# Attention kernel: causal zeros in two parts on GpSimd, and a background rate that depends on what runs

## The chip, the core and the metric

The kernel runs on one core of a Trainium2 chip. A core has five engines with queues of their own: TensorE (PE; its weight loads are shown as PEld), VectorE (DVE), ScalarE (ACT), GpSimd (POOL) and SyncE (SP, which only issues transfers here). Each works through its queue in order and waits on semaphores for the others. The metric is the device time of one execution in microseconds (us); lower is better.

## The reference, cut to what matters

Two results stand side by side in the output. The right half is a spectral filter (a 2-D real FFT of a 2048 x 576 input, a product with complex weights, the inverse FFT). The left half is an attention with a memory over four segments of 512 rows, 32 heads of 18:

```python
for s in range(N):                      # N = 4 segments of L = 512 rows
    qs, ks, vs = q[:, :, s], k[:, :, s], v[:, :, s]
    logits = jnp.einsum("bhqd,bhkd->bhqk", qs, ks) * scale + mask   # causal
    p = _softmax(logits, axis=-1)
    a_dot = jnp.einsum("bhqk,bhkd->bhqd", p, vs)
    pq = phi(qs)
    num = jnp.einsum("bhld,bhde->bhle", pq, M)                      # memory terms
    den = jnp.einsum("bhld,bhd->bhl", pq, z)[..., None] + 1e-6
    o = g * (num / den) + (1.0 - g) * a_dot
    ...
    M = M + jnp.einsum("bhld,bhle->bhde", phi(ks), vs)
    z = z + jnp.einsum("bhld->bhd", phi(ks))
return o @ wo
```

## The kernel before, in words

The first 350 us or so hold the forward FFT, the projections to q, k and v, and the inverse FFT. The change touches only the last stage, `attention`.

`attention` runs 133 steps; step t handles one head of one segment. Four heads make a quad (k = t // 4, place hh = t % 4), two quads a head group (n = k // 2), eight groups of steps, 32 in all, a segment. In a step the program writes, in this order and in alternation:

- `s1(t+11)`: the logits of the head 11 steps ahead, in three PSUM tiles, only for the row maxima (VectorE: `mg`, `mx`);
- `s2(t)`: the logits of head t, transposed, with the maxima subtracted through two added rows of the query stack; ScalarE's exponentials (L728, L733, L737) write P[0], P[1], P[2];
- `pv`: the products of the quad before with v, half of them at hh = 1 (P[0] and the last 128 columns of P[1]), half at hh = 3 (the rest of P[1], and P[2]);
- background pieces by `run_bg`, from a list of generators.

When a quad's last exponentials are issued (hh = 3), GpSimd sets the part above the diagonal to zero in four blocks (`sel`, L741). At the next step (hh = 0) `mpath` prepares the maxima of the quad two ahead: VectorE and ScalarE put them into `mg`, GpSimd splits them into two bf16 parts `mh` (L707, L708), TensorE transposes those one step later (`mt`, L711), ScalarE copies them and issues the transfer that writes them into the query stack (L717). Query stacks (Qs) stand in three buffers, key stacks in four; their transfers go out on SyncE's queue, one or two a step.

The background consists of `late_setup` (the output weight wo: SyncE loads a block into `ob`, ScalarE copies it into `woh`, GpSimd writes the rest `wol`, L650), the denominators `den` (pd, L807 and L810), `mixed` (for each of five tiles a combining piece of the segment before, L878 with VectorE's product and, from the second segment on, GpSimd's add L884; a memory piece `pn` L831; a piece `pb` L837) and `oproj` (the output projection `po`, L901, in 16 half units). All of these take their PSUM tile from one bank (`post`). `run_bg(rate)` adds the rate to an account and runs one piece when the account has reached 1; it is called twice a step, with 0 and with 1.2, so that every fifth step has two pieces. `later(k, f)` puts f at the end of the step k - 1 after the present one, seen from within a step.

The order in which instructions are written is the order of each engine's queue: nothing reorders them. The tile framework adds the semaphore waits. Transfers issued by SyncE and ScalarE use eight semaphores in turn, and each waits for the one that had its semaphore before.

Of the kernel before, what the change touches and what calls it, by code (L numbers as in the profile page):

```python
# [5 lines left out]
F32=mybir.dt.float32; F32R=mybir.dt.float32r  # L6
# [402 lines left out]
class ATT:  # L409
# [223 lines left out]
    def late_setup(s,cp):  # L633

        nc,io=s.nc,s.io; q=[]
        s.sel=cp.tile([96,5,126],BF,name="sel",bufs=1); nc.gpsimd.dma_start(s.sel,io["sel"].rearrange("p (t m) -> p t m",t=5))
        s.woh=cp.tile([128,5,576],F32R,name="woh",bufs=1); s.wol=cp.tile([128,5,576],F32R,name="wol",bufs=1)
        for t in (0,1,2,3,5,4,6):
            if t: yield
            if t<6:  # L640
                x=cp.tile([128,576],F32,name="ob"); q.append((t,x))
                nc.sync.dma_start(x,io["wo"][:,576*t:576*t+576])
            yield
            if t!=5: yield
            if len(q)>(t<6):
                u,x=q.pop(0)
                if u==5: nc.scalar.copy(s.wol[64:96,4],x[64:96]); continue
                r=128 if u<4 else 72
                nc.scalar.copy(s.woh[:,u],x)
                nc.gpsimd.tensor_tensor(s.wol[:r,u],x[:r],s.woh[:r,u].bitcast(F32),op=OP.subtract)  # L650
        yield
        yield from s.gates()
    def stack_dmas(s,n,qk):
# [65 lines left out]
    def s2(s,t):  # L719
        nc=s.nc; k,hh=divmod(t,4); n,qd=divmod(k,2); h=4*qd+hh  # L720
        Q,K=s.Qs[n%3],s.Ks[n%4]; tp=s.tp
        if hh==0: s.P[k]=[tp.tile([128,4,w],F32,name=f"P{i}") for i,w in enumerate((512,512,256))]
        P=s.P[k]
        q=lambda o: Q[:110,h,o:]
        kk=lambda j: K[:110,h,128*j:128*j+128]
        p0=s.ps.tile([128,512],F32,name="s2",tag="s2")
        nc.tensor.matmul(p0,kk(0),q(0),start=True,stop=True)  # L727
        nc.scalar.activation(P[0][:,hh],p0,AF.Exp,scale=SC)  # L728
        yield
        p1=s.ps.tile([128,512],F32,name="s2",tag="s2")  # L730
        nc.tensor.matmul(p1[:,:384],kk(1),q(128),start=True,stop=True)  # L731
        nc.tensor.matmul(p1[:,384:],kk(3),q(384),start=True,stop=True)  # L732
        nc.scalar.activation(P[1][:,hh],p1,AF.Exp,scale=SC)  # L733
        yield
        p2=s.ps.tile([128,256],F32,name="s2",tag="s2")
        nc.tensor.matmul(p2,kk(2),q(256),start=True,stop=True)  # L736
        nc.scalar.activation(P[2][:,hh],p2,AF.Exp,scale=SC)  # L737
        r=slice(0,4) if k<31 else (slice(0,3) if hh==2 else slice(3,4))
        if hh==3 or k==31 and hh==2:
            def sel(x):  # L740
                nc.gpsimd.affine_select(out=x[:,r],in_=x[:,r],pattern=[[0,r.stop-r.start],[1,128]],compare_op=OP.is_ge,fill=0.0,base=0,channel_multiplier=-1)  # L741
            sel(P[0][:,:,:128])
            sel(P[1][:,:,:128])
            sel(P[1][:,:,384:])
            sel(P[2][:,:,:128])
        yield
    def pv(s,k,jj):

# [91 lines left out]
        yield  # L840
    def mixed(s,g):

        c=s.combine(g-1)
        d=5 if g==3 else 4
        for i in range(5+d):
            next(c,None); yield
            if i>=d:
                for _ in s.mem1(g,ORD[i-d]): yield
    def ux_load(s,g,t):
        r=126 if t<4 else 72  # L850
        s.ux[t]=s.tp.tile([128,512],F32,name="ux",tag="ux",bufs=3)
        s.nc.sync.dma_start(s.ux[t][:r],s.uD[g][126*t:126*t+r])
    def combine(s,g):

        nc=s.nc; tp=s.tp; xs=s.ux
        s.oh=[None]*5; s.ol=[None]*5
        eng=lambda: nc.vector if s.now>=117 else nc.gpsimd
        yield
        yield
        def high(u):  # L860
            r=126 if u<4 else 72
            s.oh[u]=tp.tile([128,512],F32R,name="oh",bufs=5); s.ol[u]=tp.tile([128,512],F32R,name="ol",bufs=5)
            (nc.vector.tensor_copy if s.now>=119 else nc.scalar.copy)(s.oh[u][:r],s.am[u][:r])
        def low(u):
            r=126 if u<4 else 72
            A,B=s.oh[u],s.ol[u]
            l=B if u<4 else tp.tile([128,512],F32R,name="ol4",bufs=1)
            eng().tensor_tensor(l[:r],s.am[u][:r],A[:r].bitcast(F32),op=OP.subtract)
            if u==4:
                s.later(1,lambda: nc.sync.dma_start(B[:72].bitcast(F32),A[:72].bitcast(F32)))  # L870
                s.later(2,lambda: (nc.sync.dma_start(A[72:128].bitcast(F32),l[:56].bitcast(F32)),nc.sync.dma_start(B[72:88].bitcast(F32),l[56:72].bitcast(F32))))
        late=g==2
        for t in range(7+late):
            if t>1 and not late: high(ORD[t-2]); low(ORD[t-2])
            if t<5:
                i=t; t=ORD[t]; r=126 if t<4 else 72; x=xs[t]
                pb=s.post("pb")
                nc.tensor.matmul(pb[:r],s.sel[:,t,:r],s.rc["rr"],start=True,stop=True)  # L878
                if g==0:
                    s.am[t]=tp.tile([126,512],F32,name="am",bufs=5)  # L880
                    nc.vector.tensor_tensor(s.am[t][:r],x[:r],pb[:r],op=OP.mult)
                else:
                    nc.vector.tensor_tensor(x[:r],x[:r],pb[:r],op=OP.mult)
                    eng().tensor_tensor(s.am[t][:r],x[:r],s.am[t][:r],op=OP.add)  # L884
                t=i
                if t<2: s.later(1,lambda t=t: s.ux_load(g,ORD[t+3]))
            if late and 1<t<7: high(ORD[t-2])
            if late and t>2: low(ORD[t-3])
            yield
# [49 lines left out]
    def begin(s,sm,sp,ps1):  # L939
        s.late=[]; s.now=-1  # L940
        s.sm,s.sp,s.ps1=sm,sp,ps1
        s.mh=sm.tile([128,8,16],BF,name="mh",bufs=1); s.nc.gpsimd.memset(s.mh,0.0)
        s.mg={};s.mx={};s.m2={};s.P={};s.vs={};s.rc={};s.am={};s.pq={};s.ux={};s.potag=None
    def prologue(s):

        nc,io=s.nc,s.io
# [18 lines left out]
    def attention(s,tp,ps):  # L965
        nc=s.nc; s.tp,s.ps,s.psm,s.mtag=tp,ps,s.ps1,"s1"
# [18 lines left out]
        for t in range(133):  # L985
            k,hh=divmod(t,4); n,qd=divmod(k,2); g=k//8
            if hh==0 and qd==0:
                if 0<n<14: q+=s.stack_dmas(n+2,0)
                if 0<n<13: q+=s.stack_dmas(n+3,1)
                if n+2<16: q.append(lambda n=n: s.load_v(n+2))  # L990
            st=t%32
            if 16<=t<21: s.pq_load(1,ORD[t-16])
            if t==34: bg.append(s.den(1,lane))
            if st==8 and g>0:
                def ln(g=g):
                    r=s.recip(s.rD[g-1],s.rrD[g-1],s.g1,False,"rr",2)
                    for i in range(8):
                        if 2<i<6: s.ux_load(g-1,ORD[i-3])
                        next(r); yield
                    yield from r  # L1000
                    bg.append(s.mixed(g))
                    o=s.oproj(g-1)
                    if g<3: bg.append(itertools.islice(o,4)); bg.append(s.den(g+1,lane))
                    bg.append(o)
                lane.append(ln())
            if t==125: lane.append(s.recip(s.rD[3],s.rrD[3],s.g1,False,"rr"))
            a=s.s1(t+11) if t+11<128 else iter(())
            b=s.s2(t) if t<128 else iter(())
            if q: q.pop(0)()
            if qu: qu.pop(0)()  # L1010
            steps(a,1)
            steps(b,1)
            run_bg(0)
            steps(a,1)
            steps(b,1)
            if 4<=t-1<132: s.pv((t-5)//4,(t-5)%4)
            run_bg(1.2)
            steps(a,1)
            if hh==1 and m is not None: steps(m,1)
            steps(b,1)  # L1020
            if hh==1 and m is not None: steps(m,1)
            if hh==0 and k+2<32: m=s.mpath(k+2); next(m)
            if t>=7 and t%4==3:
                s.pv_out((t-7)//4)
                if t%8==3:
                    u=s.u_dmas((t-11)//8)
                    if t<124: s.later(1,lambda u=u: qu.extend(u))
                    else: qu+=u
            for l in list(lane):
                try: next(l)  # L1030
                except StopIteration: lane.remove(l)
            if q and t%8==0: q.pop(0)()
            if qu: qu.pop(0)()
            s.due(t)
# [32 lines left out]
        nc=s.nc  # L1067
# [113 lines left out]
```

## Time and profile before

| | |
|---|---|
| median of 3 runs | 703.1 us (702.56 to 704.32) |
| profiled execution | 701.82 us, span 700.1 us |
| clock granted to TensorE | 1.00 |
| attention steps | from about 352 us to the end |
| busy, share of the span | PE 97%, PEld 72%, DVE 77%, ACT 63%, POOL 28% |
| DMA | 123.81 MB, mean 177 GB/s |

The span is the time from the program's first to its last instruction; the execution's own time holds 1.7 us more. In the rows, "out<-in" are the program's tile names, the numbers in front are start and length in us (timeline) or a total, a count and the longest (waits), and what stands in brackets is the idle time before an instruction and what ended it. Idle time of an engine that nobody waits for costs nothing.

### The profile page before, as it was taken

What the parts mean: (1) busy time and instruction counts of PE and PEld (TensorE: products, weight loads), DVE (VectorE), ACT (ScalarE), POOL (GpSimd) and SP (SyncE); (2) the same over time, 40 slices, a digit from 0 to 9 for tenths busy, and PEclk for the clock granted to TensorE, in tenths of its full rate; (3) what the DMA queues carried; (4) which work ended last, traced back from release to release, by engine and by line L of the source; (5) the groups of instructions that cost most, each with busy time, mean ns of one, the idle gap of its engine ahead of it and who ended that gap; (6) DMA issues with size and microseconds to landing.
All of it is one profiled execution on the core that took longest, in us unless ns stands there. A gap on an engine that the chain in (4) does not pass through costs nothing.

```text
span 700.1 us, 14377 instructions
## 1 busy us (share of the span) xinstructions
PE 682.6 (97%) x5040; PEld 502.6 (72%) x5040; DVE 537.1 (77%) x1149; ACT 444.5 (63%) x997; POOL 192.7 (28%) x389
## 2 busy tenths in 40 slices
PE   9999999999999999999999999999999999998998
PEld 6899779879879879999954445445666445664497
DVE  5799979779689679788688888888657876567633
ACT  4677795585685483554378787777666776567531
POOL 2111000100100102655225343443323652235310
PEclk9999999999999999999999999999999999999999
DMA  9896455585466678899338976976666766442152
GB/s 342 273 287 184 134 162 188 166 240 172 122 183 206 163 199 296 196 241 265 126 113 198 200 169 148 202 199 158 151 134 170 196 166 153 101 132 68 28 153 90
DMA packets 71362, 123.81 MB, mean 177 GB/s; under 512 B 12236, under 2 KB 39530, under 8 KB 67698
## 3 DMA queue, kind: packets, MB, share of 16 engines
q1 hardware_dynamic: 64638, 106.89, 57.7%
q0 software_dynamic: 5632, 15.76, 8.1%
q8 instruction: 40, 0.66, 0.4%
q10 hardware_dynamic: 1020, 0.25, 0.2%
q14 instruction: 32, 0.26, 0.1%
HBM read 82.10 MB, written 39.81 MB: 174 GB/s over the span
## 4 chain that ended last, share of the span: by engine, by line
PE 76%; DVE 7%; DMA 6%; ACT 5%; issue 2%; POOL 2%; SPq 1%; ACTq 0%; DVEq 0%; POOLq 0%
PE s L678 10%; PE pj L485 10%; PE pv L756 10%; PE pjv L485 7%; PE po L901 6%; PE i L330 4%; PE i L319 4%; PE f L145 4%; PE s L727 3%; PE c L166 3%; PE s L731 3%; PE po L930 2%; PE pn L831 2%; PE s L691 2%; PE s L736 2%
## 5 line engine op out<-in xcount | busy, mean ns | idle before, releaser
L686 DVE CUSTOM_DVE_ANT_0 junk<-s,x 128x512 bf16<-128x512 f32 x248 | 136.8, 551 | 55.8 <-PE s L678 50.7
L741 POOL TENSOR_SCALAR_AFFINE_SELECT P<-P 128x512 f32<-128x512 f32 (+2 forms) x132 | 78.3, 625 | 110.1 <-ACT P L728 102.2
L692 DVE TENSOR_REDUCE mx<-s 128x4 f32<-128x512 f32 x128 | 87.6, 684 | 5.2 <-PE s L691 3.3
L728 ACT ACTIVATE P<-s 128x512 f32<-128x512 f32 x128 | 77.9, 608 | 10.3 <-PE s L727 3.1
L756 PE MATMUL pv<-P,vs 128*32 128x512 f32 (+3 forms) x1024 | 82.5, 439 | 0.1
L737 ACT ACTIVATE P<-s 128x256 f32<-128x256 f32 x128 | 50.0, 390 | 46.9 <-PE s L736 46.5
L733 ACT ACTIVATE P<-s 128x512 f32<-128x512 f32 x128 | 77.7, 607 | 2.4 <-PE s L732 2.2
L678 PE MATMUL s<-Ks,Qs 108*128 108x384 bf16 (+3 forms) x256 | 69.2, 301 | 1.6 <-DVE mx L692 1.2
L756 PEld LDWEIGHTS pv<-P,vs 128*32 128x32 f32 x1024 | 26.9, 109 | 45.3 <-issue 34.8
L485 PE MATMUL pj<-x,wqkh 128*128 128x512 f32 x162 | 56.3, 408 | 0.0
L231 DVE TENSOR_TENSOR Z<-Z 128x580 f32<-128x580 f32 (+2 forms) x51 | 45.9, 911 | 0.5
L678 PEld LDWEIGHTS <-Qs 108*128 108x128 bf16 x320 | 31.5, 98 | 19.1 <-issue 8.7
L691 PE MATMUL s<-tri,idb 128*128 128x128 bf16 x256 | 43.0, 219 | 0.0
L543 POOL MEMSET vt<- 128x32 f32 x16 | 2.4, 162 | 140.7 <-PE pm L553 122.8
L319 PE MATMUL i<-civ,Y 128*128 128x256 f32 (+1 forms) x288 | 39.4, 289 | 0.6 <-POOL Y L304 0.6
L504 DVE SCALAR_TENSOR_TENSOR ex<-pj,ex 128x512 f32<-128x512 f32 (+1 forms) x28 | 19.3, 688 | 24.7 <-ACT ex L502 24.7
L319 PEld LDWEIGHTS i<-civ,Y 128*128 128x128 f32 (+1 forms) x288 | 36.6, 181 | 1.6 <-POOL Y L304 1.0
L330 PE MATMUL i<-itab,T 128*128 128x290 f32 (+1 forms) x224 | 36.7, 307 | 0.1
L485 PE MATMUL pj<-xh,wqkl 128*128 128x512 f32 x90 | 35.6, 395 | 0.0
L485 PE MATMUL pj<-x,wqkl 128*128 128x512 f32 x90 | 35.6, 395 | 0.0
L485 PE MATMUL pj<-xh,wqkh 128*128 128x512 f32 x90 | 35.6, 395 | 0.0
L485 PEld LDWEIGHTS pj<-x,wqkh 128*128 128x128 f32 x162 | 30.5, 189 | 6.5
(216 smaller groups left out, 1808.1 us busy)
## 6 DMA issues: line engine op xcount, KB each, us to landing
qkD<-sp SPq DMA_DIRECT2D x32, 384.0 KB
xin<-xb SPq DMA_DIRECT2D x16, 384.0 KB
cfw<-cfw POOLq DMA_DIRECT2D x16, 384.0 KB, 4.2
civ<-civ POOLq DMA_DIRECT2D x16, 384.0 KB, 9.1
vs<-vD SPq DMA_DIRECT2D x16, 330.0 KB
vD<-vt SPq DMA_DIRECT2D x16, 311.0 KB
W<-w SPq DMA_DIRECT2D x16, 290.0 KB
yb<-yout SPq DMA_DIRECT2D x16, 290.0 KB
```

The costliest lines, as they stand in the source:

```text
L319: nc.tensor.matmul(p[:m,k],Y[i][:,q,c*128:c*128+m],cc[:,hl,o:o+256],start=n==0,stop=n==5)
L330: nc.tensor.matmul(p,x,t,start=n==0,stop=n==6)
L485: s.nc.tensor.matmul(out,a,b,start=i==0,stop=i==len(L)-1)
L678: nc.tensor.matmul(out,Q[:108,h,128*i:128*i+128],K[:108,h,:128*(i+1)],start=True,stop=True)
L686: nc.vector.tensor_tensor_reduce(out=junk[:,:w],in0=src,in1=s.mask[:,512-w:],scale=1.0,scalar=-3.0e38, op0=OP.add,op1=OP.max,accum_out=s.m ...
L691: nc.tensor.matmul(pa[:,o+w-128:o+w],s.idb,s.tri,start=False,stop=True,skip_group_check=True)
L692: nc.vector.tensor_reduce(out=s.mx[k][:,hh],in_=pa.rearrange("p (b c) -> p b c",c=128),axis=mybir.AxisListType.X,op=OP.max)
L728: nc.scalar.activation(P[0][:,hh],p0,AF.Exp,scale=SC)
L733: nc.scalar.activation(P[1][:,hh],p1,AF.Exp,scale=SC)
L737: nc.scalar.activation(P[2][:,hh],p2,AF.Exp,scale=SC)
L741: nc.gpsimd.affine_select(out=x[:,r],in_=x[:,r],pattern=[[0,r.stop-r.start],[1,128]],compare_op=OP.is_ge,fill=0.0,base=0,channel_multiplie ...
L756: nc.tensor.matmul(s.pvt[32*hh:32*hh+32,128*j:],vt[:,j,19*h:19*h+32],mv[0][:,hh,mv[1]],start=j==0,stop=j>1,skip_group_check=True)
```

## The change

Four edits. Two of a quad's four zeros (the first 128 columns of P[1], and P[2]) are written at the end of the next step, behind the two parts of the maxima; the last quad keeps all four together. The subtraction for `wol` goes to the end of its step, and `late_setup` has one piece more for each of five blocks. The add on GpSimd in the combining piece goes to the end of the step where that step is the first of a quad, for the second segment only. The background's rate is 1.0 while `mixed` runs for segments 1 and 2, 1.35 after that, and 1.2 before the first and from the last one on.

```diff
                 nc.scalar.copy(s.woh[:,u],x)
-                nc.gpsimd.tensor_tensor(s.wol[:r,u],x[:r],s.woh[:r,u].bitcast(F32),op=OP.subtract)
+                s.later(1,lambda u=u,x=x,r=r: nc.gpsimd.tensor_tensor(s.wol[:r,u],x[:r],s.woh[:r,u].bitcast(F32),op=OP.subtract))
+                yield
...
             sel(P[0][:,:,:128])
-            sel(P[1][:,:,:128])
             sel(P[1][:,:,384:])
-            sel(P[2][:,:,:128])
+            def rest():
+                sel(P[1][:,:,:128])
+                sel(P[2][:,:,:128])
+            if k<31: s.rest=rest
+            else: rest()
...
     def mixed(s,g):
+        s.rate=1.0 if g<3 else 1.2
         c=s.combine(g-1)
         d=5 if g==3 else 4
         for i in range(5+d):
             next(c,None); yield
             if i>=d:
                 for _ in s.mem1(g,ORD[i-d]): yield
+        if g<3: s.rate=1.35
...
                     nc.vector.tensor_tensor(x[:r],x[:r],pb[:r],op=OP.mult)
-                    eng().tensor_tensor(s.am[t][:r],x[:r],s.am[t][:r],op=OP.add)
+                    f=lambda t=t,x=x,r=r,e=eng(): e.tensor_tensor(s.am[t][:r],x[:r],s.am[t][:r],op=OP.add)
+                    f() if eng() is nc.vector or s.now%4<3 or g==2 else s.later(1,f)
...
-            run_bg(1.2)
+            run_bg(s.rate)
...
             if hh==0 and k+2<32: m=s.mpath(k+2); next(m)
+            if hh==0 and s.rest: s.rest(); s.rest=None
```

What this does to the queues is shown at three places. GpSimd around step 16, where the last block of the output weight is split; AFFINE_SELECT are the zeros in P, CAST and TENSOR_TENSOR on mh the maxima's two parts. Before:

```order
L741 AFFINE_SELECT P0_4689<-P0_4689 128x4x128
L741 AFFINE_SELECT P1_4690<-P1_4690 128x4x128 x2
L741 AFFINE_SELECT P2_4691<-P2_4691 128x4x128
L650 TENSOR_TENSOR wol_4298<-ob_4703,woh_4297 72x576
L707 CAST mh_3126<-mg_4719 128x16
L708 TENSOR_TENSOR mh_3126<-mg_4719,mh_3126 128x16
```

And now, from the second block of the same quad to the last of the next one (the lines of the changed program are one or more higher; _4684 and _4685 are the quad that was _4690 and _4691, _4831 to _4833 the next):

```order
L742 AFFINE_SELECT P1_4684<-P1_4684 128x4x128
L708 CAST mh_3126<-mg_4713 128x16
L709 TENSOR_TENSOR mh_3126<-mg_4713,mh_3126 128x16
L742 AFFINE_SELECT P1_4684<-P1_4684 128x4x128
L742 AFFINE_SELECT P2_4685<-P2_4685 128x4x128
L742 AFFINE_SELECT P0_4831<-P0_4831 128x4x128
L742 AFFINE_SELECT P1_4832<-P1_4832 128x4x128
L708 CAST mh_3126<-mg_4864 128x16
L709 TENSOR_TENSOR mh_3126<-mg_4864,mh_3126 128x16
L742 AFFINE_SELECT P1_4832<-P1_4832 128x4x128
L742 AFFINE_SELECT P2_4833<-P2_4833 128x4x128
L650 TENSOR_TENSOR wol_4298<-ob_4837,woh_4297 72x576
```

The split stood between zeros and maxima; now the maxima's parts follow two zeros, the other two come behind them, and the split is a quad later.

TensorE in step 56, the first place where the rates differ: L727 (L728 now) is the first product of `s2`, L878 (L884) a combining piece, L831 a memory piece. Before:

```order
L727 MATMUL s2_6336<-Qs1_3134,Ks3_3138 128x512
L878 LDWEIGHTS sel_4295
L878 MATMUL pb_6343<-rr_6043,sel_4295 126x512
L678 LDWEIGHTS Qs2_3135
L678 MATMUL s1_6347<-x0_2608,Qs2_3135 128x512
L731 LDWEIGHTS Ks3_3138
L731 MATMUL s2_6351<-Qs1_3134,Ks3_3138 128x384
L732 LDWEIGHTS Ks3_3138
L732 MATMUL s2_6351<-Qs1_3134,Ks3_3138 128x128
L831 MATMUL pn_6355<-pq_4864,Mst1_64 126x512
```

And now:

```order
L728 MATMUL s2_6334<-Qs1_3134,Ks3_3138 128x512
L679 LDWEIGHTS Qs2_3135
L679 MATMUL s1_6337<-x0_2608,Qs2_3135 128x512
L732 LDWEIGHTS Ks3_3138
L732 MATMUL s2_6341<-Qs1_3134,Ks3_3138 128x384
L733 LDWEIGHTS Ks3_3138
L733 MATMUL s2_6341<-Qs1_3134,Ks3_3138 128x128
L884 LDWEIGHTS sel_4295
L884 MATMUL pb_6349<-rr_6043,sel_4295 126x512
```

The combining piece moved to the second place in the step, and the memory piece left the step; it comes in step 57.

SyncE around step 16: ob<-wo is a block of the output weight, Qs1 the query stack of head group 4, uD the PV results going out, x0 one more of the stacks, vs the values, pq the input of the memory pieces. Before:

```order
L642 DMA ob_4703<-wo 128x576
L772 DMA uD0_3143<-U_4534 18x2x512
L660 DMA x0_2608<-qkD1_71 16x4096
L772 DMA uD0_3143<-U_4534 18x2x512 x2
L662 DMA x0_2608<-reD1_75 12x4096
L772 DMA uD0_3143<-U_4534 18x2x512
L669 DMA vs_4787<-vD0_81 128x4x165
L801 DMA pq_4827<-pqD1_78 72x512
L660 DMA Qs1_3134<-qkD1_71 48x4096
L660 DMA Qs1_3134<-qkD1_71 32x4096
```

And now:

```order
L670 DMA vs_4784<-vD0_81 128x4x165
L805 DMA pq_4822<-pqD1_78 72x512
L661 DMA Qs1_3134<-qkD1_71 48x4096
L642 DMA ob_4837<-wo 128x576
L661 DMA Qs1_3134<-qkD1_71 32x4096
L805 DMA pq_4861<-pqD1_78 126x512
L661 DMA Qs1_3134<-qkD1_71 16x4096
```

The last block of the weight, which stood ahead of the PV results of the group before, now stands between the first and the second piece of the query stack.

More of the change, by code (lines that the diff above doesn't have):

```diff
@@ L942, in begin @@
         s.mh=sm.tile([128,8,16],BF,name="mh",bufs=1); s.nc.gpsimd.memset(s.mh,0.0)
-        s.mg={};s.mx={};s.m2={};s.P={};s.vs={};s.rc={};s.am={};s.pq={};s.ux={};s.potag=None
+        s.mg={};s.mx={};s.m2={};s.P={};s.vs={};s.rc={};s.am={};s.pq={};s.ux={};s.rate=1.2;s.potag=s.rest=None
     def prologue(s):
```

## The prediction

> **What bounds the kernel now.** I read the page first, then the windows by stage, then TensorE's waits, then the timeline at each wait. The page:
>
> ```profile
> span 700.1 us, 14377 instructions
> PE 682.6 (97%) x5040; PEld 502.6 (72%) x5040; DVE 537.1 (77%) x1149; ACT 444.5 (63%) x997; POOL 192.7 (28%) x389
> ```
>
> TensorE is busy nearly always, so time comes back only where it waits. The change acts from 352 us, where the attention steps begin, to about 652 us. The windows of that part, without stretches in which TensorE has next to no idle time:
>
> ```profile
> core 0: us, PE busy (x) PEld busy (x) DVE busy (x) ACT busy (x) POOL busy (x), PEclk, DMA share, GB/s
> 352.40:380.00 27.60, 25.91 (x229) 13.33 (x226) 23.81 (x67) 22.57 (x54) 14.24 (x24) 1.00 0.62 149
> 380.00:435.00 55.00, 53.53 (x501) 27.60 (x501) 45.22 (x142) 42.57 (x104) 20.30 (x42) 1.00 0.78 174
> 447.00:485.00 38.00, 37.12 (x312) 18.63 (x309) 31.57 (x94) 28.59 (x67) 16.81 (x30) 1.00 0.78 188
> 545.00:590.00 45.00, 43.42 (x356) 22.61 (x347) 35.18 (x102) 32.34 (x76) 26.11 (x38) 1.00 0.72 167
> 634.50:652.00 17.50, 15.43 (x116) 6.46 (x114) 12.37 (x25) 13.04 (x32) 9.09 (x14) 1.00 0.22 66
> ```
>
> Length less PE busy gives 1.69 + 1.47 + 0.88 + 1.58 + 2.07 = 7.7 us of idle time, the size of what can be won. The clock is 1.00 throughout. Who ended the idle time (TensorE's waits, 350 to 660 us; columns: total us, times, longest):
>
> ```profile
> PE mt L711 <- POOL mh L708: 2.2, 5, 0.8
> PE s L727 <- ACT P L728: 1.2, 5, 0.3
> PE pn L831 <- DVE am L881: 0.7, 1, 0.7
> PE pn L831 <- DVE ux L883: 0.6, 1, 0.6
> PE pb L878 <- DVE ux L883: 0.5, 1, 0.5
> PE mt L711 <- DVE mg L686: 0.5, 1, 0.5
> PE pb L878 <- DVE am L838: 0.3, 1, 0.3
> ```
>
> Two kinds stand out: the maxima's transpose L711, which waits for GpSimd's two parts of mh, and a memory or combining matmul (L831, L878) that waits until VectorE has emptied the one PSUM bank that these pieces share. A wait costs more than its gap, because the shown end of a matmul overlaps the next one:
>
> ```profile
> 420.84 0.28 PE L678 MATMUL s<-Ks,Qs 108*128 108x256 bf16 x1
> 420.96 0.22 PE L711 MATMUL mt<-idb,mh 128*128 128x128 bf16 x1
> ...
> 388.85 0.23 PE L711 MATMUL mt<-idb,mh 128*128 128x128 bf16 x1 [0.81 <-POOL mh L708]
> ```
>
> Without a wait the transpose starts 0.12 after a matmul that is shown as 0.28 long, so 0.16 is to be added to each gap.
>
> [...] By the PEld column (18.63 of 38.00 at 447 to 485 us) half of TensorE would be free and such a change could win far more. The start-to-start spacing of 0.12 without any gap, above, contradicts that for these stages, and I go by gaps.
>
> **The change part by part.**
>
> *Zeros behind the maxima, and the splits of the output weight (L650) behind both.* What holds mh, on GpSimd:
>
> ```profile
> 386.95 1.41 POOL L650 TENSOR_TENSOR wol<-ob,woh 72x576 fp32r<-72x576 f32 x1 [0.79 <-ACT woh L649]
> 388.30 0.19 POOL L707 CAST mh<-mg 128x16 bf16<-128x16 f32 x1
> ...
> 425.27 2.40 POOL L741 TENSOR_SCALAR_AFFINE_SELECT P<-P 128x512 f32<-128x512 f32 x4 [4.91 <-ACT P L728]
> 428.86 0.20 POOL L707 CAST mh<-mg 128x16 bf16<-128x16 f32 x1 [1.20 <-DVE mg L704]
> ...
> 560.27 1.27 POOL L884 TENSOR_TENSOR am<-ux,am 126x512 f32<-126x512 f32 x1
> ```
>
> In a plain quad (425 us) the four zeros end 1.2 us before mh could start, so moving two of them wins nothing. It wins where GpSimd has a split (1.41) or an add (1.27) as well: there mh starts the moment GpSimd is free (388.30, no idle time in the row). Now 1.2 us of zeros (half of 2.40) and, but for one quad, the split stand behind mh; in the quad where a split stays ahead, two zeros less make up 1.2 of its 1.41. The deferred adds do the same for the wait at 562 us. The six maxima waits are 2.2 + 0.5 + 6 x 0.16 = 3.7 us; I take all as gone. What is late next in a plain quad is the maximum itself (the 1.20 <-DVE above), and TensorE does not wait for that.
>
> The moved zeros are read by the second half of the PV products, two steps after their new place: mh ends some 0.5 us after its start (388.30 to the transpose at 388.85), so at about 429.4 in the plain quad, the zeros would end at 430.6, and that half starts at 432.55:
>
> ```profile
> 428.63 1.28 PE L756 MATMUL pv<-P,vs 128*32 128x512 f32 x16
> ...
> 432.41 0.22 PE L732 MATMUL s<-Qs,x 110*128 110x128 bf16 x1
> 432.55 1.28 PE L756 MATMUL pv<-P,vs 128*32 128x384 f32 x16
> 433.77 0.28 PE L678 MATMUL s<-Ks,x 108*128 108x256 bf16 x1
> ```
>
> That leaves 2 us of cover; one add or split (1.27 to 1.41) still fits. Each half now has a semaphore wait of its own on TensorE, some 60 more; the first half (428.63) has had such waits and takes the same 1.28. To the 0.01 us of the rows that leaves 0 to 0.6 us for all; I take nothing.
>
> *One piece a step beside memory terms.* The four bank waits, 0.7 + 0.6 + 0.5 + 0.3 + 4 x 0.16 = 2.7 us, all stand where two pieces fell into one step. With one a step VectorE has at least a step to empty the bank, and I take them as gone. VectorE is not short of time there: 31.57 of 38.00 and 35.18 of 45.00.
>
> *1.35 beside the projection.* It makes up for the slower pieces before: the same matmuls end one step later than before, and nothing waits for that step. But the denominators' matmuls (pd) move from a step with PV products to one without, where less overlaps:
>
> ```profile
> 422.07 0.22 PE L732 MATMUL s<-Qs,x 110*128 110x128 bf16 x1
> ...
> 423.44 0.28 PE L678 MATMUL s<-Ks,Qs 108*128 108x256 bf16 x1
> ...
> 504.49 0.22 PE L732 MATMUL s<-Qs,x 110*128 110x128 bf16 x1
> 506.93 0.28 PE L678 MATMUL s<-Ks,Qs 108*128 108x256 bf16 x1
> ```
>
> Alone they take at most 423.44 - 422.07 = 1.37; beside PV the stretch is 2.44, less 1.36 for PV alone (432.41 to 433.77), so 1.08. Less some 0.05 of ordinary spacing, they cost 0.24 more, in two places: 0.5 us.
>
> *The output weight's loads, which move with the splits.* SyncE's queue now has the sixth of them between the pieces of the query stack of head group 4. That stack, and where TensorE first reads it:
>
> ```profile
> 384.00:395.00 11.00, 9.97 (x90) 5.33 (x89) 8.95 (x30) 8.55 (x22) 5.77 (x11) 1.00 0.97 198
> 384.31 0.78 SPq L660 DMA_DIRECT2D Qs<-qkD  x2
> 386.45 0.37 SPq L662 DMA_DIRECT2D Qs<-reD  x1
> 394.49 0.32 PE L678 MATMUL s<-x,Qs 108*128 108x384 bf16 x1 [0.21 <-issue]
> ```
>
> The DMA engines are full (0.97), and TensorE waits a little, for no engine, exactly at the first matmul that reads the new stack. I read this as the stack landing last. Then the 0.97 us won at 388.85 is lost again at 394.49, for the stack lands when it lands; and 288 KB more ahead of its end are 1.5 us at 198 GB/s. Bounds: 0, if that gap is something else, to 2.4. I take the 0.97 and half of the 1.5, 1.7 us, since SyncE will have less queued from the steps before.
>
> *New waits among the single pieces*: 0 to 1.2 (two of the four bank waits come back elsewhere); I take 0.3, the shortest row.
>
> Sum: -3.7 - 2.7 + 0.5 + 1.7 + 0.3 = -3.9 us. The profiled execution took 701.8 us, 700.1 of span and 1.7 around it, 1.3 under the median of 703.1; the waits are no part of that difference that I can see, so the sum goes on the median: **699.2 us**.
>
> **The rivals.** About 0.3% (2.1 us) is what a measurement of this kernel tells from no change, so "same" is 701.0 to 705.2.
>
> *The time is taken back* (0.18): the stack costs its full 2.4, and of the other waits 2.7 us return because VectorE's or ScalarE's queue, emptied by TensorE's pauses until now, is next in line. For it: ScalarE is the releaser of five waits (1.2 us) that the change leaves alone. Against: no idle time at 412 to 435 us, a stretch with the same base load. -6.4 + 0.5 + 2.4 + 2.7 = -0.8: 702.3 us.
>
> *Slower: ScalarE waits on the transfers' rotation* (0.13). The transposed maxima are written to Qs by a transfer that ScalarE issues (L717), 30 times. In the built program it waits for a semaphore that eight transfers ago had, and SyncE's order, which the change shuffles, decides which that is. Two such waits show now:
>
> ```profile
> 391.81 0.62 ACTq L717 DMA_DIRECT2D x<-mts  x1
> 392.48 0.60 ACT L728 ACTIVATE P<-s 128x512 f32<-128x512 f32 x1 [1.33 <-DMA pq<-pqD]
> ...
> 403.06 0.38 PE L727 MATMUL s<-x,Ks 110*128 110x512 bf16 x1 [0.24 <-ACT P L728]
> ```
>
> ScalarE lost 1.33 at the first; after the second one TensorE lost 0.24 + 0.16 = 0.40. Every exponential queues behind that issue. It decides from the point where the transfer eight places back lands after ScalarE's turn, as where a stack or an add-bound ux load stands there. It takes 6.0 us to pass 705.2 from 699.2: 15 more at 0.40, or 5 at the full 1.33. At eight, at the mean of 0.87: 699.2 + 7.0 = 706.2 us.
>
> *Slower: the moved zeros and VectorE block each other* (0.03). They now run beside VectorE's maxima and multiplications; 31 quads, 1.2 us each, half of it felt, would be 18.6: 717.8 us. Against it:
>
> ```profile
> 424.82 0.68 DVE L686 CUSTOM_DVE_ANT_0 junk<-s,x 128x512 bf16<-128x512 f32 x1
> 427.36 0.68 DVE L686 CUSTOM_DVE_ANT_0 junk<-s,x 128x512 bf16<-128x512 f32 x1
> ```
>
> The second ran while the zeros of 425.27 to 427.67 did, the first did not: 0.68 both. [...]
>
> **How the numbers follow.** My forecast has 0.66, and all of that is faster; the first rival (0.18) is "same"; the two slower ones have 0.16. The low end is everything removed, nothing given back but the 0.5, and the 1.2 of the exponentials' waits gone too: 703.1 - 5.9 - 1.2 = 696.0. The high end takes in the first rival and the upper bound of the new waits, 702.3 + 1.2 = 703.5; what lies above is the slower cases, 0.16.
>
> **What would show it right or wrong.** Right: the waits of L711 for GpSimd all but gone; no wait of L831 or L878 over 0.3 at the new places; a longer gap than 0.21 where the stack of group 4 is first read; pd with 1.3 us alone. Wrong: ScalarE idle behind L717 at many quads (slower), the second half of PV waiting for L741, or L711 now waiting for VectorE's maxima.

## The result, and the profile after

The changed kernel takes 705.53 us (median of 22 runs, 701.52 to 708.81) against 702.3 us for the kernel before on the same chips (22 runs, 700.22 to 704.32): 1.0039 of it, with a 95% interval of 1.0027 to 1.005. It is slower, by 2.7 us by this ratio and by 3.2 us by the two medians, where 699.2 was forecast. The profiled execution took 704.09 us. Its page, and the windows of the stretches that the prediction listed:

```profile
span 702.4 us, 14384 instructions
PE 684.6 (97%) x5040; PEld 503.1 (72%) x5040; DVE 537.2 (76%) x1149; ACT 444.5 (63%) x997; POOL 192.2 (27%) x389
```

```profile
core 0: us, PE busy (x) PEld busy (x) DVE busy (x) ACT busy (x) POOL busy (x), PEclk, DMA share, GB/s
352.40:380.00 27.60, 26.73 (x241) 14.52 (x240) 24.57 (x70) 23.62 (x58) 12.97 (x23) 1.00 0.58 142
380.00:435.00 55.00, 51.16 (x456) 25.68 (x455) 41.66 (x130) 39.70 (x96) 19.59 (x38) 0.94 0.79 168
545.00:590.00 45.00, 43.16 (x355) 21.64 (x353) 36.31 (x105) 33.70 (x80) 24.71 (x36) 1.00 0.75 178
```

From 352 to 380 us the idle time fell as forecast (27.60 less 25.91 before, less 26.73 now). From 380 to 435 us it rose from 1.47 to 3.84, and the granted clock, 1.00 before, is 0.94. TensorE's waits from 350 us on (total us, times, longest), the two longest groups and that of the maxima's parts:

```profile
PE s L728 <- ACT P L729: 4.1, 5, 3.2
PE s L679 <- DMA Ks<-qkD: 1.6, 1, 1.6
...
PE mt L712 <- POOL mh L709: 0.9, 2, 0.6
```

The waits for the maxima's parts went from 2.7 us to 0.9, and the bank waits that the prediction listed are gone. In their place stand one gap of 3.2 and one of 1.6. The first one, in the timeline:

```profile
383.45 0.36 SPq L805 DMA_DIRECT2D pq<-pqD  x1
392.05 0.62 ACTq L718 DMA_DIRECT2D x<-mts  x1
392.72 0.60 ACT L729 ACTIVATE P<-s 128x512 f32<-128x512 f32 x1 [4.77 <-DMA pq<-pqD]
393.37 0.38 PE L728 MATMUL s<-Qs,Ks 110*128 110x512 bf16 x1 [3.17 <-ACT P L729]
395.49 0.48 PE L679 MATMUL s<-x,Qs 108*128 108x384 bf16 x1 [0.67 <-DVE mg L705]
```

ScalarE ran nothing for 4.77 us, because the issue of the maxima's transfer (L718) stood in its queue until 392.05: the semaphore still belonged to the pq load of 383.45, whose updates end at 391.98. No exponential ran meanwhile, so TensorE found no free bank and idled 3.17 us. It is the wait that the prediction quoted at 391.81 with 1.33; the issue goes out at the same moment as before (392.05 against 391.81), only TensorE stands earlier in front of it. Then the clock:

```profile
392.00:396.00 4.00, 1.96 (x10) 0.91 (x10) 1.21 (x5) 3.25 (x7) 1.22 (x2) 0.74 0.95 176
396.00:400.00 4.00, 4.00 (x25) 1.27 (x24) 1.39 (x3) 1.90 (x6) 2.96 (x5) 0.50 0.82 179
400.00:404.00 4.00, 4.00 (x37) 2.17 (x35) 3.30 (x12) 2.97 (x7) 0.65 (x2) 0.90 0.57 161
```

Half the clock is granted for about 7 us ((0.26 + 0.50 + 0.10) x 4 us, doubled): 25 matmuls in 396 to 400 us, where the kernel before has 45.

The starts of the steps (the first product of `s2`, 512 columns) show where the time went. Each number is the start of a step less the start of the same step before, both counted from their own step 0, in us; minus is ahead of before. At the steps shown all these kernels have the same number of matmuls behind them. Each row is the one profiled execution of a kernel: that of e8 was 3.2 us above the median of its runs, that of e9 1.7 below.

| kernel | 10 | 18 | 20 | 22 | 50 | 82 | 114 | 126 |
|---|---|---|---|---|---|---|---|---|
| changed | -0.55 | -2.49 | 0.84 | 4.05 | 3.48 | 3.15 | 3.20 | 3.40 |
| e1 rates alone | -0.01 | -0.02 | -0.02 | 0.14 | 0.42 | 0.27 | 0.67 | 3.65 |
| e2 rate 1.2 | -0.54 | -2.48 | 1.97 | 3.21 | 3.25 | 3.80 | 3.58 | 3.58 |
| e3 pq in 26-30 | -0.56 | -2.50 | -2.50 | -2.28 | -1.27 | -1.48 | -1.75 | -1.54 |
| e5 no extra piece | -0.55 | -1.74 | 1.76 | 2.73 | 2.15 | 1.84 | 3.90 | 4.12 |
| e6 zeros alone | -0.56 | 0.51 | 2.12 | 2.23 | 1.74 | 2.30 | 2.29 | 2.31 |
| e7 L718 on GpSimd | -0.78 | -2.72 | -2.72 | 4.25 | 3.73 | 3.41 | 3.37 | 3.58 |
| e8 pq in 22-26 | -0.55 | -2.48 | -2.48 | -2.35 | 3.45 | 3.60 | 5.48 | 5.69 |
| e9 pq in 0-4 | -0.54 | -2.48 | -2.48 | -2.68 | -3.26 | -3.58 | -4.10 | -3.90 |
| e13 before, pq in 0-4 | -0.05 | -0.05 | -0.05 | -0.42 | -1.00 | -0.68 | -0.69 | -0.70 |
| e15 split alone | -0.54 | -2.48 | 0.99 | 4.00 | 3.50 | 3.68 | 3.66 | 3.67 |

The changed kernel gains 2.49 us by step 18 and loses 6.54 from there to step 22: 3.33 at ScalarE's wait (step 20), 1.07 more up to step 21, with the stack's first read, and 2.14 from there on under half clock.

The second gap of the list stands 180 us later, again where a query stack is first read:

```profile
561.13 1.36 SPq L661 DMA_DIRECT2D Qs<-qkD  x3
563.75 0.37 SPq L663 DMA_DIRECT2D Qs<-reD  x1
571.61 0.32 PE L679 MATMUL s<-Ks,Qs 108*128 108x384 bf16 x1 [1.60 <-DMA Ks<-qkD]
```

The row names a key stack's load, but the matmul reads the stack whose loads are shown above it: their semaphore updates end at 571.25, and TensorE's weight load of the stack starts at 571.57.

### The profile page after: what moved, and what is told of

Its sections match the earlier page's. It is cut to its first block, busy times and chain, and to the rows that moved or that the text cites. A ratio compares the mean times of both kernels' runs of the same rounds, so it can differ in the third digit from the quotient of the medians.

```text
span 702.4 us, 14384 instructions
## 1 busy us (share of the span) xinstructions
PE 684.6 (97%) x5040; PEld 503.1 (72%) x5040; DVE 537.2 (76%) x1149; ACT 444.5 (63%) x997; POOL 192.2 (27%) x389
## 4 chain that ended last, share of the span: by engine, by line
PE 75%; DVE 9%; ACT 5%; DMA 5%; issue 3%; POOL 2%; SPq 1%; ACTq 0%; DVEq 0%; POOLq 0%
PE pv L760 10%; PE s L679 10%; PE pjv L485 8%; PE pj L485 8%; PE po L908 7%; PE i L319 4%; PE i L330 4%; PE s L728 3%; PE s L732 3%; PE po L937 2%; PE f L145 2%; PE s L692 2%; PE c L166 2%; PE pn L835 2%; PE s L737 2%
## 5 line engine op out<-in xcount | busy, mean ns | idle before, releaser
L742 POOL TENSOR_SCALAR_AFFINE_SELECT P<-P 128x512 f32<-128x512 f32 (+2 forms) x132 | 78.9, 621 | 78.6 <-ACT P L729 76.8
```

## The experiments

Theory A: ScalarE's wait at L718, with the half clock that follows, is the loss. Theory B: the new rates are. Rival C: the query stack itself is late there, and the pq load is only first in line. Rival D: the weight's block that moved into the stack is the cause. The times of each run are compared with the kernel before on the same chip.

**e1, rates alone, and e2, the rest without the rates.**

```diff
 e1 (kernel before):   + s.rate=1.0 if g<3 else 1.2 ... if g<3: s.rate=1.35 ... run_bg(s.rate)
 e2 (changed kernel):  - s.rate=1.0 if g<3 else 1.2 ... - if g<3: s.rate=1.35
```

> The kernel before with nothing but the new rates (1.0 beside the memory terms, 1.35 beside the projection). Theory A (the loss is at 388 to 400 us: ScalarE stands in front of the issue of the maxima's transfer L718, whose semaphore a pq load still holds; TensorE idles 3.2 us and is then granted half clock for several us): nothing changes ahead of the first memory terms, so no half clock beyond the last 1 us (mean 1.00) and 702.0 us, that is 0.3 under before (the four bank waits, 2.5, against a late stack near 570 us, 1.8, and the denominators, 0.5). Theory B (the rates lose the time, since background pieces and their loads come later and run into the stack loads): 703.5 or more, 1.2 over before or worse.

> The changed kernel with the old rate of 1.2 throughout; zeros, split and adds stay changed. Theory A: everything up to 435 us is as in the changed kernel, ScalarE's 4.8 us wait for a pq load and the half clock stay, 705 us, at most 0.7 from the changed kernel. Theory B: the loss goes with the rates, 700 us.

e1: 705.58, ratio 1.0043 (1.0026 to 1.0059). e2: 704.62, 1.0026 (1.0009 to 1.0044). The rates by themselves lose as much as the whole change, the rest by itself two thirds of it. In e2 it is the same place (gap 4.29, then half clock: 0.72 granted in 396 to 400 us), as A said. In e1 that place is untouched (0.14 at step 22), and A's 702.0 missed. There the maxima wait for GpSimd, since the zeros and the adds still stand ahead of them: 5.0 us in seven waits, against 2.2 in five before (its waits, the longest one in the timeline, and a window behind that):

```profile
PE mt L711 <- POOL mh L708: 5.0, 7, 1.5
```

```profile
641.08 0.23 PE L711 MATMUL mt<-idb,mh 128*128 128x128 bf16 x1 [1.47 <-POOL mh L708]
```

```profile
643.00:647.00 4.00, 4.00 (x20) 1.16 (x20) 1.87 (x3) 1.68 (x4) 1.81 (x3) 0.57 0.44 140
```

Half clock again, at 643 us behind a gap of 1.47. So neither theory holds alone: by these waits the rates need the other edits, and these run into the transfers.

**e3 and e4, the pq loads ten steps later; e8, six.**

```diff
-            if 16<=t<21: s.pq_load(1,ORD[t-16])
+            if 26<=t<31: s.pq_load(1,ORD[t-26])      (e8: 22<=t<27; e9, e13: 0<=t<5)
```

> The changed kernel with the five pq loads for the second segment's denominators issued in steps 26 to 30 in place of 16 to 20 (they are read from step 34 on). The transfer that has the semaphore before the maxima's transfer in step 19 is then an earlier one. Theory A: ScalarE does not wait there (below 0.5 us), TensorE has no gap over 1.5 us at 385 to 400, the clock is 1.00, and the time is 700 us, 5 under the changed kernel. Rival C (TensorE would wait for the query stack itself in that place, so the pq load is only the first in line): the gap moves to the first read of the stack, 2 us or more there, and the time is 703 to 705.

> The control for the run with the later pq loads: the kernel before with the same move. Theory A: its 1.33 us wait of ScalarE near 391 us was covered and TensorE gains nothing much: 701.5 to 702.5, within 0.8 of before. If the loads as such are what costs time (less traffic beside the stack), it gains 1.5 or more as well.

> The changed kernel with the pq loads in steps 22 to 26: later than the stack of group 4, and ahead of that of group 6, into which those of steps 26 to 30 ran. Theory A: no wait of ScalarE over 1 us at 385 to 400, and the 1.3 us that the stack of group 6 cost near 415 us is gone: 700 us, 1.3 under the run with steps 26 to 30. If the loads only push another stack (that of group 5, read near 410 us), the gap stands there and the time is 701 to 702.

e3: 701.3, 0.9981 (0.9961 to 1.0), 4.2 under the changed kernel; the lead of 2.50 passes step 22. e4, the control: 701.75, 0.9987 (0.9971 to 1.0003). A and C both allow this: with fewer loads in front, ScalarE's wait and the late stack go together. e8 missed: 704.12, 1.0029 (1.0008 to 1.0051). With the pq loads beside the next stack, the gap stood at that stack, whose last load landed at 411.33, and the clock was halved from 410.1 on (0.76 granted in 408 to 412 us):

```profile
411.68 0.48 PE L679 MATMUL s<-Ks,Qs 108*128 108x384 bf16 x1 [3.04 <-DMA Ks<-qkD]
```

**e7, the maxima's transfer issued by GpSimd.**

```diff
-        else: s.later(2,lambda: nc.scalar.dma_start(out,mt))
+        else: s.later(2,lambda: nc.gpsimd.dma_start(out,mt))
```

> The changed kernel with the maxima's transfers (L718) issued by GpSimd in place of ScalarE; nothing else is moved, and the output weight and the pq loads stay where the change put them. Theory A: ScalarE no longer stands before a transfer's semaphore, no gap over 1.5 us in TensorE at 385 to 400, clock 1.00, 700 us. Rival C (the query stack itself is late there): a gap of 2 us or more at its first read and 703 to 705. A new cost may appear on GpSimd, whose queue then holds the issue and its wait for ScalarE's copy ahead of zeros or maxima: up to 1 us more.

706.64, 1.0059 (1.0039 to 1.008), above what either expected. The place of the gap decides between A and C. ScalarE waits no more, step 20 is still 2.72 ahead, and then (timeline, and the window behind):

```profile
396.15 0.50 PE L679 MATMUL s<-x,Qs 108*128 108x384 bf16 x1 [4.74 <-DMA Qs<-reD]
```

```profile
396.00:400.00 4.00, 3.85 (x20) 1.42 (x24) 1.39 (x3) 1.28 (x3) 0.30 (x1) 0.50 0.87 180
```

The whole loss moved to the first read of the stack. ScalarE's wait was first in line, not the cause: theory A falls, C stands.

The stack's lateness can also be read without any wait, from the semaphore updates in the traces. The table has the last update of the stack's loads and the first matmul that reads the stack, in us from each kernel's own step 0:

| | before | changed | e6 | e7 | e3 | e8 | e9 | e13 |
|---|---|---|---|---|---|---|---|---|
| last load landed | 42.25 | 43.87 | 44.35 | 44.21 | 40.17 | 40.11 | 39.62 | 41.09 |
| first read | 42.45 | 44.15 | 44.55 | 44.26 | 40.26 | 40.20 | 39.87 | 42.09 |

In all but e13 the read stands 0.05 to 0.28 behind the landing, in the kernel before too: there was no room left for a lead. In the changed kernel the stack even lands 1.62 later than before. Where the pq loads are out of the way it lands early enough for TensorE to keep the lead.

**e5, e6 and e15: the weight's loads where they were, zeros alone, split alone.**

```diff
 e5 (changed kernel):  -                yield      (late_setup's extra piece)
 e6 (kernel before):   only the two zeros moved behind the maxima's parts
 e15 (kernel before):  only  + s.later(1,lambda ...: nc.gpsimd.tensor_tensor(s.wol...))  + yield
```

> The changed kernel without the extra piece that late_setup has for each block, so that the output weight's loads stand in SyncE's queue where they stood before, ahead of the query stack of group 4; the splits still go to the end of their step. The semaphore before the maxima's transfer of step 18 still belongs to a pq load. Theory A (TensorE's lead of 3 us meets a transfer that lands when it lands): the pq load lands some 1.5 us earlier at most, ScalarE still waits 3 us or more, TensorE's gap is 1.5 to 2.5, with or without half clock behind it: 702.5 to 704.5. Rival D (the weight's block in the middle of the stack is what costs the time): the gap is below 0.5 and the time 700.

> The kernel before with nothing but two of the four zeros behind the maxima's parts. Theory A: the waits of L711 for GpSimd at 371 to 389 us go (1.9 us with what a gap costs beyond itself), the lead meets the pq load, ScalarE waits 3 us or more there and TensorE 1.5 to 3; the bank waits stay: 703 to 705. Against A: the removed waits stay removed, 700.5.

> The kernel before with nothing but the split of the output weight at the end of its step and late_setup's extra pieces. Theory C: the waits of L711 for GpSimd at 371 to 389 us shrink since no split stands ahead of the maxima's parts, a lead of 1 to 2 us forms, and it is given back to the transfers at 385 to 400 us, with half clock if the gap comes to 3 us: 702.5 to 704.5. If the lead stays, 701.

e5: 705.89, 1.0045 (1.0025 to 1.0065), with the gap below; rival D falls. The time is above the 702.5 to 704.5 of the expectation too, since the second stack cost 2.06 there as well (from step 82 to 114), by the numbers with half clock again: the profile's mean clock of 0.995 is some 7 us at half clock over the span of 704.2, and the windows of 392 to 400 us hold only 3.4 of them. The gap:

```profile
394.59 0.59 PE L727 MATMUL s<-Qs,Ks 110*128 110x512 bf16 x1 [3.35 <-ACT P L728]
```

e15: 704.23, 1.0017 (1.0003 to 1.0031). The split alone makes the whole early lead (2.48 at step 18) and loses it the same way (4.00 at step 22, gap 3.32). e6: 704.18, 1.002 (1.0006 to 1.0034), the time expected but by another way. The zeros alone give no lead: the 0.55 that is won at step 9 is gone by step 18, with a stack's first read at step 13 and with ScalarE late at steps 16 and 17, and 1.6 more goes at step 20, where ScalarE is late at the issue of the maxima's transfer as in the changed kernel. The weight's block stands where it stood before, and the stack of group 4 still lands late (44.35 in the table), so the block is not what delays it. The granted clock is 1.00 in this profile: e6 loses time without any half clock.

```profile
377.12 0.32 PE L678 MATMUL s<-Ks,x 108*128 108x384 bf16 x1 [0.90 <-DMA x<-reD]
384.53 0.38 PE L727 MATMUL s<-Qs,Ks 110*128 110x512 bf16 x1 [0.45 <-ACT P L728]
395.40 0.38 PE L727 MATMUL s<-Qs,Ks 110*128 110x512 bf16 x1 [1.46 <-ACT P L728]
```

The adds were not tried alone.

**e9 to e13: loads out of the way.** Five steps lie between the one in which a stack's buffer comes free and the first read of the new stack, and for the stack of group 4 the DMA engines are full in that time. The windows of the changed kernel, one ahead and one with the stack of group 4:

```profile
360.00:368.00 8.00, 8.00 (x78) 4.30 (x77) 6.80 (x22) 6.81 (x17) 4.21 (x8) 1.00 0.22 56
384.00:395.00 11.00, 7.66 (x68) 3.66 (x66) 6.95 (x22) 6.13 (x16) 2.81 (x6) 0.95 1.00 196
```

The DMA share is 0.22 in the first and 1.00 in the second, so loads that aren't urgent belong ahead.

```diff
 e9, e10, e12 (changed kernel), e11, e13 (kernel before):  + if 0<=t<5: s.pq_load(1,ORD[t])
 e10, e11, e12: late_setup with one piece (before), two (changed) for a block in place of three and four
 e12: + s.rate=1.0 if g<2 else 1.2 ... + if g<2: s.rate=1.35
```

> The changed kernel with the five pq loads in steps 0 to 4 (352 to 360 us, where the DMA engines are 0.3 to 0.7 busy) in place of 16 to 20. Theory C, as the runs so far leave it (the stack of a head group can only be loaded from the step in which its buffer comes free, five steps before its first read, and the DMA engines are full there; what TensorE saves in those steps it gives back when the stack lands, and a gap of some 3 us costs half clock on top): 1.2 MB less beside the stacks of groups 4 to 6, so no gap over 1.5 us at 385 to 420, clock 1.00, the lead of 3 us stays, 699.5 us. Theory A' (only the transfer that ScalarE waits for matters): also 699.5 here. Against both: 702 or more.

> The control for the best version so far: the kernel before with the pq loads in steps 0 to 4. Theory C: the kernel before has only small waits on transfers to lose, so it wins 0.3 to 1.0 (the 0.2 us gap and the slow steps near 394 and 403 us): 701.5 to 702.3. The change is then worth 1.5 to 2.5 us once those loads are out of the way. If the loads alone make the 2.7 us of that version, it comes to 700 and the change is worth nothing even there.

e9: 699.93, 0.9962 (0.9949 to 0.9976): the lead is 2.68 at step 22 and 3.26 at step 50, at a granted clock of 1.00. Its windows at the two places:

```profile
384.00:395.00 11.00, 10.88 (x103) 5.42 (x101) 9.78 (x30) 10.02 (x24) 3.91 (x11) 1.00 0.94 208
557.00:573.00 16.00, 14.90 (x122) 7.47 (x119) 12.24 (x36) 11.20 (x26) 9.71 (x15) 1.00 0.89 201
```

e13, the control, missed its expectation: 700.68, 0.9968 (0.9958 to 0.9979). The early loads alone win 2.4 us by the medians. Its profiled run shows only 0.70 of that in the attention, and in it the stack is no longer what TensorE waits for (landed 41.09, read 42.09). Another 0.70 lies ahead of the attention, where the kernels are the same: step 0 starts anywhere from 351.02 to 352.84 in the profiles. The rest I could not place, since one execution of the kernel before was profiled, and it was one of the faster (701.82 against 702.3). The nine runs of e13 lie closer together (700.21 to 701.77) than the 21 of before (701.55 to 704.41), which fits a transfer that is sometimes late. By the ratios e9 and e13 cannot be told apart. Their profiled runs differ by 3.2 us at step 126 and by 2.2 in all, but that of e9 (698.22) is the fastest of its five.

> As the run with pq loads in steps 0 to 4, and late_setup without two of its pieces for each block, so that the six blocks of the output weight are loaded by about 371 us in place of 383. Theory C: another 0.6 MB leave the stretch from 370 us on; with the early loads the DMA engines have room for what TensorE gains, 699.0 us, at or a little under the run without it. If the denser splits on GpSimd hold the maxima's parts, L711 waits for GpSimd again below 370 us, up to 1.5 us in all.

> The control: the kernel before with the same two moves of loads, zeros, splits, adds and rates as before. Theory C: the kernel before has no lead to lose, its stacks land in time or nearly so, and the loads alone win 0.5 us or less, or lose up to 2 since splits now crowd the first steps ahead of the maxima: 702 to 704. The difference to the changed kernel with the same loads is then what the change is worth where the transfers are out of the way: 3 to 5 us. If instead the loads alone bring it to 700 or below, the change itself is worth little even so.

> As the changed kernel with both moves of loads, but with the new rates only for the first of the two segments (1.2 from the second one on). In the changed kernel the second segment won 2.5 us of bank waits and lost 1.8 of them to the stack of group 13 near 571 us and the rest to pieces that cost more beside PV products. Theory C: the second segment comes out the same with either rate, within 0.5 us of the run with all rates. If single pieces are worth their waits there, it is 2 us slower.

e10: 702.41, 0.9999 (0.9984 to 1.0015); e11: 705.58, 1.0039 (1.0023 to 1.0054); e12: 706.23, 1.0041 (1.0021 to 1.0061). The denser blocks backfired: ScalarE now reaches a block's copy before the block has landed, and steps 3 to 8 pay for it, again with half clock (timeline and windows of e10):

```profile
359.15 0.67 ACT L647 CAST woh<-ob 128x576 fp32r<-128x576 f32 x1 [1.66 <-DMA ob<-wo]
```

```profile
360.00:368.00 8.00, 7.48 (x43) 3.42 (x43) 3.71 (x11) 4.89 (x12) 5.43 (x8) 0.57 0.45 129
```

The profiled run of e10 (706.11) is the slowest of its twelve. By the medians e10 is 3.2 us ahead of e11, but that is not a price of the change: the kernel before has its blocks denser still (one piece against two), and in the profiled runs e11 has lost 6.99 by step 10 and e10 4.54. e12 against e10 is 3.8 slower, not within 0.5 as expected; its profile has other gaps in the second segment and the end than e10's, so I don't read a price of the rates from it.

**e14 and e16: fewer bytes ahead of the second stack.**

```diff
-        if g<3: s.later(1,lambda: s.pq_load(g+1,t))
+        if g<3: s.later(4,lambda: s.pq_load(g+1,t))     (e14 from e9, e16 from e13)
```

> As the changed kernel with pq loads in steps 0 to 4, and the later pq loads (those that a memory piece requests for the next segment) issued three steps later, so that 252 KB less stand ahead of the end of the stack of group 13. Theory C: TensorE's gap of 1.0 us at the first read of that stack, near 566 us, shrinks by the 1.0 to 1.3 us that these bytes take at 200 GB/s: 698.8 to 699.3. If that gap has another cause, it stays, and the time with it.

> The control for the fastest version: the kernel before with both moves of pq loads (steps 0 to 4, and the later ones three steps later), without any of the change. Where the loads alone make the time, it comes to 698.6 like the changed kernel with them; where the change is worth its removed waits once the stacks have room, it stays near the 700.7 of the kernel before with early pq loads, 2 us above.

e14: 698.61, 0.9938 (0.9923 to 0.9954), the fastest of all. Its profiled run (700.47, the slowest of its six) still has a gap at that stack, 1.6 us, so the reason expected was not seen. e16, the control: 700.95, 0.9962 (0.9948 to 0.9977). With both moves of loads the change is worth 1.7 us by the ratios (0.9962 less 0.9938), though the intervals still overlap a little.

## Why the prediction was wrong

- **The maxima's waits (-3.7): right in kind, nearly in size.** The three of steps 9 to 17 went, and the lead was 2.49 by step 18. That of step 1 stayed (0.24), that of 117 grew (0.42 to 0.62), and the one at 562 us is gone. e15 shows that the splits made the early lead, not the zeros.
- **The bank waits (-2.7): right.** None is left. But from step 82 to 114 the changed kernel came out 0.05 behind instead of 1.9 ahead (0.60 + 0.47 + 0.33 + 3 x 0.16, the waits of before in these steps), as the stack of group 13 took 1.76 (1.60 + 0.16), a stack that the prediction did not look at: waits that it removed stood in or ahead of its five steps.
- **Denominators (+0.5): right**, 1.26 alone (2.54 - 1.28) in step 72 against 1.03 beside PV (3.68 - 2.65).
- **"The query stack gives back 1.7, bounds 0 to 2.4": the step that failed.** It measured 6.54, in three parts. The lead: all 2.49 us won ahead of the stack came back, where the term counted only the 0.97 of the last wait. The stack itself: counted from step 0 its first load went out 1.5 us earlier than before (its last one 0.2 later), yet it landed 1.62 later and its first read came 1.70 later, where the term had 0.75, half of the weight's block. So "the stack lands when it lands" was right in that TensorE has to wait for it, but its landing moved. The block does not explain that (e5, e6); why it lands later stays open. The clock: the other 2.35, from the first read to step 22, were lost under half clock, and for this the prediction had no term at all.
- **New waits (+0.3) and zeros against VectorE: no price seen.** Of new waits for the moved zeros the list after has one, of PV for L742, 0.2 us.
- **The rivals.** "The time is taken back" (0.18) had the direction, at 702.3, with the stack at 2.4 and without the clock. The rival on ScalarE's semaphores (0.13) named the instruction and the place and came closest, 706.2, but by eight places of 0.87; it was one of 4.77, and e7 shows that taking it away saves nothing. That its number is near is luck.

What the clock cost: the mean granted clock of the 22 runs goes from 1.000 (701.52 us, one run) over 0.998 (702.15 to 706.12, five runs) to 0.992 (706.78 and 707.7). A straight line through them has 586 us for a clock of 1, so 2.9 us for 0.005, and 702.7 at full clock, which is where the kernel before stands (702.3). It is a fit over scattered runs (correlation 0.71), not a run in which the clock alone was changed. By the line alone the removed waits were given back to the transfers, and the half clock made the slowdown. The profiled run says less: of the 4.05 us that it is behind at step 22, 2.35 are the half clock and 1.70 the later stack, and e6 is slower than before (1.002) with a clock of 1.000 in eight of its twelve runs.

## What to carry to other kernels

Where buffers rotate, look up for every load the step that frees its buffer and the step that reads it. If the DMA engines are full between the two (a share of 1.00 in 384 to 395 us here), waits removed there came back at the read in this kernel, however well they were removed; first move other loads out of that stretch (here five early loads won 2.4 us without any other change, and 4.4 us with the change and one more move). And where the granted clock falls behind a stall on TensorE, price both the stall and the slow clock (here 2.35 us behind a gap of 3.17; behind the gap of 1.60 at 571 us the clock stayed at 1.00).

## What was not expected of the hardware

- A gap of 3.17 us on TensorE was followed by half clock for 6.83 us (0.50 granted from 393.94 to 400.76 us), at which step 21 took 4.78 us where it takes 2.65. The gap of 1.60 at 571 us was not (1.00 granted in 569 to 575 us).
- But e1 lost the clock at 643 us with no gap over 1.47 (0.57 granted in 643 to 647 us); 1.48 of the 3 us ahead (640 to 643) were busy:

```profile
640.00:643.00 3.00, 1.48 (x9) 0.71 (x10) 1.14 (x3) 1.55 (x5) 2.16 (x4) 1.00 0.41 111
```

  So here half clock also followed a stretch that was half idle, with no long gap in it.
- In the traces of the two kernels the clock records change only at whole multiples of 3.41 us from the first one: at 114, 116 and 204 in the changed kernel, at 204 in the kernel before. The rows are stretches of that length, two right before a fall (changed kernel, e1) and two that kept the full clock (changed kernel, at its gap of 1.60, and e9):

```profile
390.53:393.94 3.41, 0.57 (x3) 0.27 (x3) 0.40 (x1) 1.22 (x3) 0.55 (x1) 1.00 0.98 192
639.91:643.32 3.41, 1.80 (x13) 0.82 (x13) 1.54 (x3) 1.87 (x5) 2.25 (x4) 1.00 0.43 123
567.99:571.40 3.41, 2.01 (x12) 0.85 (x9) 2.45 (x9) 2.73 (x7) 3.34 (x5) 1.00 1.05 210
280.36:283.77 3.41, 1.87 (x16) 1.67 (x16) 3.31 (x5) 2.41 (x7) 2.82 (x3) 1.00 0.70 187
```

  TensorE was busy for 0.17 and 0.53 of the first two and for 0.59 and 0.55 of the others. Four rows don't show what decides between the two cases, and no run here moved a gap against these stretches.
